# Attention in pairs of heads with plain fp32 products on halves of TensorE's array, the first block's x taken from PSUM, and two-operation bit joins

## The chip, the cores and the metric

The program runs on one core of one Trainium2 chip. The metric is the device time of one execution in microseconds. A core has five engines that work side by side and wait for each other through semaphores: PE (TensorE, the matrix products), ACT (ScalarE), DVE (VectorE), POOL (GpSimd) and SP (SyncE, which here only issues transfers). Products read SBUF and write PSUM, which has eight banks of 512 fp32 columns on 128 partitions.

## The reference

Attention for 4 batches and 8 heads over 576 positions of width 64, mixed with a memory read-out, then two feed-forward layers over 2304 rows. Inputs q, k, v are fp32, some inputs are scaled by 8, and the weights of both layers come as 64-bit floats.

```python
B, H, S, D = q.shape                                    # 4, 8, 576, 64
scores = q @ k.transpose(0, 1, 3, 2) / np.sqrt(D)       # causal mask, then softmax
a = softmax(np.where(causal, -1e9, scores))
local = a @ v
q_p = phi(q)                                            # x if x > 0 else exp(x) - 1, plus 1
mem_out = (q_p @ M_prev) / ((q_p * z_prev).sum(-1) + 1e-6)
x = g * mem_out + (1 - g) * local                       # g = sigmoid(beta), per head
x = x.transpose(0, 2, 1, 3).reshape(B * S, H * D)       # 2304 x 512
h = x @ w_in                                            # first layer, 512 x 2048
y = (s * np.maximum(h, 0) ** 2 + b) @ w_out             # 2048 x 512
h2 = y @ w_in2                                          # second layer
out = (h2 * np.tanh(softplus(h2))) @ w_out2             # 2304 x 512
```

## The kernel before

A planner in the kernel (class `Plan`) orders the work. Each step names its engine, an estimated duration, a priority, the buffers that it reads and writes, and its code. `order` plays the steps in time: each engine takes the ready step with the smallest priority number, and a step whose buffers have no free place in their ring waits. The outcome is a fixed order of instructions on every engine. While the program runs, each engine keeps that order and waits where it has to. While nothing else is ready for PE early on, the planner inserts products of zeros (`zero_product`).

Attention is done head by head (`unit`). The memory read-out is put in front of the scores: 64 columns of phi(q), divided by their norm, stand ahead of the probabilities, and M stands ahead of v, so that one weighting product does both. A head has 640 padded rows in five tiles of 128: the first half, TA, is tiles 0 to 2, the second half, TB, is tiles 3 and 4. For each tile PE makes the scores, DVE subtracts from the mask and takes the row minimum, ACT takes the exponential with its row sum, POOL, DVE or ACT scale by the reciprocal of the sum. PE then turns the tile in 128 x 128 pieces (transposes against `ident`), ACT copies the turned pieces out of PSUM, and PE weights v with them. The result goes to `x_d` in DRAM.

The eight heads of batch 0 ("early") use plain fp32 products: scores over rows 0 to 63 (L534), weighting into 64 columns (L624, 128\*64 in the rows). Their first halves come first, then their second halves. The other 24 heads split every operand into a high and a low part of type fp32r on ACT and DVE (L509 to L513, L601, L604, L646, L647), and use two full-width products for each (L538, L539, and L624 with 128\*128 in the rows); a last DVE operation adds the two halves of the result (L635).

The first layer (`first`, `y_part`) works in blocks of x: five small ones of 256 rows and two large ones of 512 (`NBIG`). Three products of fp32r parts stand for one exact product. `load_x` fetches a block of x from DRAM, ACT makes its high part, DVE its low part (L822 to L824). A small block handles two of the sixteen pieces of the hidden layer at a time. Large blocks use buffers (`m2a`) that open only when the last attention step is done. `rank1` gives the first layer priority numbers between those of the heads.

The weights come as 64-bit floats. `convert` loads a piece of 512 per partition, ACT scales the upper and the lower words, DVE shifts the one (L705), isolates a sign in 16-bit halves (L707, and a custom operation L709), and ACT and DVE cut the sum into high and low parts (L715, L718). There are 32 pieces for each layer. The second layer (`hidden`, L1009, and `out_block`, L1075) uses a seven-product scheme for blocks of 768 rows.

## Time and profile before

| | before |
|---|---|
| time, median of 3 runs | 1022.97 us (1022.23 to 1026.45) |
| profiled execution, its own time | 1022.02 us |
| span of that execution | 1020.2 us |
| PE busy | 996.6 us, 6742 products |
| DVE busy | 829.3 us |
| ACT busy | 697.7 us |
| POOL busy | 204.0 us |
| PE clock granted, mean | 0.998 of full speed |

Products are pipelined, and their ends are modelled: a row of the trace shows when a product starts and how long it is under way, and the time that one takes from PE is the distance to the next start. A plain fp32 product appears as two instructions of the same size, an fp32r product as one. The span runs from the first to the last instruction; the time of the execution has 1.8 us more.

### The profile page before, as it was taken

The numbers are of one execution on the slowest core, as the hardware profiler recorded it, in microseconds if no ns is written. First come the engines' busy times: TensorE is split into PE (matmuls) and PEld (weight loads), VectorE is DVE, ScalarE is ACT, GpSimd is POOL, SyncE is SP. The second block draws the span as 40 slices with busy tenths as digits, with TensorE's granted clock in tenths as the row PEclk, the third lists the DMA queues.
The fourth block names the chain that finished last, engine by engine and source line by source line (L and its number), as shares of the span: only waits on it lengthen the run. The fifth ranks groups of instructions, "written<-read, shape, count | busy, mean of one in ns | idle before, by whom it ended". The sixth has DMA issues, their size and how long they took to land.

```text
span 1020.2 us, 19909 instructions
## 1 busy us (share of the span) xinstructions
PE 996.6 (98%) x6742; PEld 926.6 (91%) x6742; DVE 829.3 (81%) x2308; ACT 697.7 (68%) x1511; POOL 204.0 (20%) x330
## 2 busy tenths in 40 slices
PE   6899999999999999999999999999999999999998
PEld 5668799998999999999888888899999999999998
DVE  7899899999999989976789975379965789667864
ACT  6888897788877877766779987456643466434552
POOL 6752133444333334310000000000010000100000
PEclk9999999999999999999999999999999999999999
DMA  9855553324323432217899985368677665766464
GB/s 252 219 174 164 174 161 94 105 90 120 128 85 92 129 93 87 86 37 250 263 285 312 316 266 178 136 241 267 201 281 243 219 215 191 261 218 222 145 223 170
DMA packets 88661, 188.60 MB, mean 185 GB/s; under 512 B 8432, under 2 KB 62704, under 8 KB 81264
## 3 DMA queue, kind: packets, MB, share of 16 engines
q1 hardware_dynamic: 81072, 135.95, 42.8%
q0 software_dynamic: 7056, 51.38, 14.9%
q8 instruction: 53, 0.87, 0.3%
q14 instruction: 48, 0.39, 0.1%
q10 hardware_dynamic: 432, 0.01, 0.0%
HBM read 144.32 MB, written 42.99 MB: 184 GB/s over the span
## 4 chain that ended last, share of the span: by engine, by line
PE 67%; issue 18%; DMA 5%; DVE 4%; ACT 3%; POOL 2%; SPq 0%; POOLq 0%; DVEq 0%; ACTq 0%
PE bank L801 18%; PE bank L879 18%; PE bank L1009 9%; PE bank L1075 6%; PE bank L624 6%; PE bank L596 4%; PE bank L534 2%; PE bank L538 2%; DMA x_d<-xs 2%; PE bank L539 1%; POOL Pt L569 1%; DMA woh<-wo_split_d 1%; PE bank L1250 1%; DMA woh<-wi_split_d 1%; DMA wih<-in_w_in 1%
## 5 line engine op out<-in xcount | busy, mean ns | idle before, releaser
L1075 PE MATMUL bank<-woh,S 128*128 128x256 f32 x792 | 107.4, 283 | 1.8 <-DMA woh<-wo_split_d 1.8
L1075 PEld LDWEIGHTS bank<-woh,S 128*128 128x128 f32 x792 | 100.8, 192 | 1.9 <-issue 1.9
L1075 PE MATMUL bank<-wol,S 128*128 128x256 f32 x720 | 98.1, 283 | 0.0
L552 ACT ACTIVATE Pt<-Pt,mx 128x64 f32<-128x64 f32 (+4 forms) x148 | 81.4, 551 | 22.5 <-DVE mx L543 22.4
L555 POOL TENSOR_SCALAR Pt<-ex,nm 128x64 f32<-128x64 f32 x148 | 73.3, 513 | 116.3 <-PE bank L596 44.9
L1009 PE MATMUL bank<-wi,woh 128*128 128x384 f32 x426 | 94.0, 335 | 0.3 <-DMA woh<-wi_split_d 0.3
L1075 PEld LDWEIGHTS bank<-wol,S 128*128 128x128 f32 x720 | 91.8, 192 | 0.0
L990 POOL DMA_DIRECT2D wol<-wo_split_d x17 | 9.2, 540 | 357.5 <-DVE wi L730 265.7
L1009 PE MATMUL bank<-wi,wol 128*128 128x384 f32 x294 | 76.0, 335 | 0.6 <-DMA wol<-wi_split_d 0.6
L1009 PEld LDWEIGHTS bank<-wi,woh 128*128 128x128 f32 x426 | 75.6, 188 | 1.0 <-DMA woh<-wi_split_d 0.5
L596 PE MATMUL bank<-ident,Pt 128*128 128x128 f32 x432 | 64.9, 276 | 7.1 <-POOL Pt L569 6.2
L604 DVE TENSOR_TENSOR PTl<-bank,PTh 128x128 fp32r<-128x128 f32 (+1 forms) x144 | 64.1, 481 | 3.1 <-ACT PTh L601 2.5
L543 DVE CUSTOM_DVE_ANT_0 Pt<-bank,mask 128x320 f32<-128x320 f32 (+3 forms) x148 | 59.3, 419 | 6.4 <-PE bank L534 3.1
L569 POOL TENSOR_SCALAR Pt<-Pt,rs 128x64 f32<-128x64 f32 (+2 forms) x68 | 51.9, 801 | 60.0 <-DVE rs L574 36.9
L596 PEld LDWEIGHTS bank<-ident,Pt 128*128 128x128 f32 x432 | 48.7, 140 | 13.6 <-POOL Pt L569 9.2
L601 ACT CAST PTh<-bank 128x128 fp32r<-128x128 f32 (+1 forms) x144 | 54.1, 432 | 5.9 <-PE bank L596 4.6
L1009 PEld LDWEIGHTS bank<-wi,wol 128*128 128x128 f32 x294 | 53.0, 188 | 1.1 <-DMA wol<-wi_split_d 0.9
L801 PE MATMUL bank<-xh,wi 128*128 128x256 f32 x320 | 51.2, 288 | 1.5 <-ACT xh L823 1.4
L879 PE MATMUL bank<-gh,wol 128*128 128x256 f32 x320 | 52.3, 287 | 0.0
L879 PE MATMUL bank<-gl,woh 128*128 128x256 f32 x320 | 52.2, 287 | 0.0
L879 PE MATMUL bank<-gh,woh 128*128 128x256 f32 x320 | 52.0, 285 | 0.0
L624 PE MATMUL bank<-PTh,V 128*128 128x384 f32 (+1 forms) x192 | 48.1, 278 | 0.0
(279 smaller groups left out, 2851.8 us busy)
## 6 DMA issues: line engine op xcount, KB each, us to landing
wol<-wo_split_d POOLq DMA_DIRECT2D x17, 1024.0 KB, 5.2
woh<-wo_split_d POOLq DMA_DIRECT2D x16, 1024.0 KB, 5.5
qk<-in_qk SPq DMA_DIRECT2D x24, 608.0 KB, 3.9
stage<-in_w_out SPq DMA_DIRECT2D x23, 512.0 KB, 4.7
wo_split_d<-high SPq DMA_DIRECT2D x44, 256.0 KB, 4.9
stage<-in_w_in SPq DMA_DIRECT2D x21, 512.0 KB, 5.2
stage<-wi_d SPq DMA_DIRECT2D x24, 384.0 KB, 4.7
wi_split_d<-woh SPq DMA_DIRECT2D x8, 1024.0 KB, 4.8
```

Of the source, the lines that this page charges most:

```text
L543: nc.vector.tensor_tensor_reduce(Pt[t].t[:, D + lo:D + hi], ps.t[:, :hi - lo], mask[:, SP - w + lo:SP - w + hi], -SCALE, mx.t[:, t:t + 1] ...
L552: nc.scalar.activation(Pt[t].t[:, D:w + D], Pt[t].t[:, D:w + D], AF.Exp, bias=mx.t[:, t + i:t + i + 1], scale=-1.0, accum_out=rs.t[:, t:t ...
L555: add(POOL, 0.3, lambda: nc.gpsimd.tensor_scalar(Pt[t].t[:, :D], ex.t[:, t, :], nm.t[:, t:t + 1], 1.0, op0=ALU.mult, op1=ALU.mult), [ex, n ...
L569: (nc.vector if e == DVE else nc.gpsimd).tensor_scalar(x, x, r, None, op0=ALU.mult)
L596: nc.tensor.transpose(ps.t[:, c - c0, :], Pt[t].t[:, c * P:(c + 1) * P], ident)
L601: (nc.vector.tensor_copy if dve else nc.scalar.copy)(PT[0].t[:, at_], ps.t[:, :n])
L604: nc.vector.tensor_tensor(PT[1].t[:, at_], ps.t[:, :n], PT[0].t[:, at_].bitcast(F32), op=ALU.subtract)
L624: nc.tensor.matmul(o.rearrange("p (t q) -> p t q", q=P), v, x.t[:, f[0]:f[-1] + 1:f[1] - f[0] if len(f) > 1 else 1, :], start=(c == 0 and ...
L801: nc.tensor.matmul(ph, w_at(nm, r, cc)[:, o:o + P], x_at(x, cc), start=(begin and part == 0 and cc == 0), stop=(part == 2 and cc == NCC - ...
L879: nc.tensor.matmul(acc[ec // per].t[:, (ec % per) * n:(ec % per + 1) * n], w_at(nm, fc // FPR, fc % FPR)[:, ec * P:(ec + 1) * P], t(x)[:, ...
L1009: nc.tensor.matmul(ps.t[:, :H2], w[i // 4].t[:, j, kk, i % 4], x[kk].t[:, k], start=begin and part == kk == 0, stop=part == 2 and kk == 1, ...
L1075: nc.tensor.matmul(acc[t].t[:, :DH], s.t[:, j, t * P:(t + 1) * P], x.t[:, k, q % 4], start=q == part == 0, stop=q == NQ2 - 1 and part == 2)
```

## The change

`unit` gives way to `pair`, which does one half (TA or TB) of two heads. All attention now uses plain fp32 products. The q and k of the pair's first head lie on partitions 0 to 63, those of the second on 64 to 127, and each score step issues one product for each head into its own bank (L526). The weighting writes the first head to partitions 0 to 63 and the second to 64 to 127 of one bank, product by product in turn (L603). The splits of operands and of results are gone. The halves come in the order TA of the four pairs of batch 0, and then by turns TB of one pair and TA of the pair four places on (the next batch); the first ten halves use weight buffers that are not yet needed (`PLACE`, `STAGED`), the others their own.

For TA of batch 0, ACT and DVE make the high and low part of the first 256 rows of x straight from the bank (L614, L615), and the first block of the first layer reads these; only rows 256 to 319 go to DRAM. First-layer priority numbers are now 500 and up (`RANK1`), all behind attention on PE, and zero products end with the first product of the first layer (`fill_end`). There are three small and three large blocks. The conversion joins sign, upper and lower words with two operations that each do a bit operation and a second one (L667, L669) where there were three. The reduction of phi(q) with z takes one product and one sum for two heads where each tile had an operation of its own.

```diff
-    NBIG = 2
+    NBIG = 3
@@ pair, in place of unit: scores
+                def mm(lo=lo, hi=hi, ps=ps, t=t):
+                    for i in range(2):
+                        nc.tensor.matmul(ps[i].t[:, :hi - lo], qkt(t * P, P)[rows(i)], kt(lo, hi - lo)[rows(i)], start=True, stop=True)
...
-                        nc.tensor.matmul(ps.t[:, :hi - lo], lhs, B1.t[:, lo:hi], start=True, stop=False)
-                        nc.tensor.matmul(ps.t[:, :hi - lo], lhs, B2.t[:, lo:hi], start=False, stop=True)
@@ pair: turning and weighting
+                def turn(ps=ps, tcs=tcs, i=i):
+                    for x, (t, c) in enumerate(tcs):
+                        nc.tensor.transpose(ps.t[:, x, :], at_t(i, t, c * P, (c + 1) * P), ident)
...
+        def mm():
+            for c in range(last + 1):
+                ts = [t for t in g if t >= c]
+                f = [at_[t, c] for t in ts]
+                cols = slice((ts[0] - lo_t) * P, n)
+                for i in range(2):
+                    nc.tensor.matmul(pv.t[rows(i), cols].rearrange("p (t q) -> p t q", q=P), vx()[:, i, c, :],
+                                     PT[i].t[:, f[0]:f[-1] + 1:f[1] - f[0] if len(f) > 1 else 1, :],
+                                     start=(c == 0), stop=(c == last))
...
+        if b == 0 and lo_t == 0:
+            k = N1
+            xh, xl = xs_[0][0][0], xs_[0][1][0]
+            half = Buf()
+            add(ACT, act_us(k), lambda: nc.scalar.copy(xh.t[:, p], pv.t[:, skip:skip + k]), [pv], [half], [xh])
+            add(DVE, dve_us(k), lambda: nc.vector.tensor_tensor(xl.t[:, p], pv.t[:, skip:skip + k], xh.t[:, p].bitcast(F32),
+                                                                op=ALU.subtract), [pv, half], [first_x[p]], [xh, xl])
@@ convert
-        add(DVE, 0.335, prio, lambda: nc.vector.tensor_scalar(w.t, w.t, 3, None, op0=ALU.logical_shift_left), [w], [w])
-        add(DVE, 0.335, prio, lambda: nc.vector.tensor_scalar(limbs()[:, :, 1], limbs()[:, :, 3], 0x8000, None, op0=ALU.bitwise_and),
-            [raw, low_words], [signed])
-        add(DVE, 0.75, prio, lambda: nc.vector.tensor_tensor(w.t, w.t, words()[:, :, 0], op=ALU.add), [raw, signed, w], [w])
+        add(DVE, 0.6, prio, lambda: nc.vector.scalar_tensor_tensor(words()[:, :, 0], words()[:, :, 1], -2 ** 31, words()[:, :, 0],
+                                                                   op0=ALU.bitwise_and, op1=ALU.bitwise_or), [raw, low_words], [signed])
+        add(DVE, 0.6, prio, lambda: nc.vector.scalar_tensor_tensor(w.t, w.t, 3, words()[:, :, 0], op0=ALU.logical_shift_left,
+                                                                   op1=ALU.bitwise_or), [raw, signed, w], [w])
@@ order of the halves
+    halves_ = [(0, p, TA) for p in range(H // 2)]
+    for i in range(B * H // 2):
+        halves_.append((*divmod(i, H // 2), TB))
+        if i + H // 2 < B * H // 2:
+            halves_.append((*divmod(i + H // 2, H // 2), TA))
+    for i, x in enumerate(halves_[:STAGED]):
+        pair(x[0], x[1], STEP * i, x[2], PLACE[i % len(PLACE)], i < H // 2 and i % 2 == 1)
...
-        return UNIT0 + UNIT * (i + LEAD) / PER_UNIT
+        return RANK1 + i
...
     plan.fill = (7.0, 85.0, 0.12, zero_product)
+    plan.fill_end = in_steps[0][0]
```

PE where the first layer begins, in the order before. L534 are scores, L1250 products of zeros, L624 a weighting, L801 the first layer; PTl and vx are the turned probabilities and the values of a second half of batch 0, xh is the block loaded from DRAM.

```order
L534 MATMUL bank_113<-qk_849 128x256
L1250 MATMUL bank_109<-zeros 128x256 x3
L624 MATMUL bank_112<-PTl_937,vx_831 64x256 x4
L624 MATMUL bank_112<-PTl_937,vx_831 64x128
L801 MATMUL bank_106<-xh_961,wi_196 128x256 x4
```

The same place now. L603 is the weighting of the fourth pair's first half, two heads by turns, L526 are scores of a second and of the next first half, L1215 zeros, L762 the first layer.

```order
L603 MATMUL bank_110<-PT_686,wol_0_185 64x384
L603 MATMUL bank_110<-PT_695,wol_0_185 64x384
L603 MATMUL bank_110<-PT_686,wol_0_185 64x256
L603 MATMUL bank_110<-PT_695,wol_0_185 64x256
L603 MATMUL bank_110<-PT_686,wol_0_185 64x128
L603 MATMUL bank_110<-PT_695,wol_0_185 64x128
L526 MATMUL bank_113<-qk_230 128x256
L526 MATMUL bank_111<-qk_230 128x256
L1215 MATMUL bank_109<-zeros 128x256 x4
L762 MATMUL bank_106<-xh_358,wi_219 128x256 x4
L526 MATMUL bank_112<-wih_0_350 128x192
L526 MATMUL bank_110<-wih_0_350 128x192
```

The first product of the first layer has moved from behind the weightings of all eight first halves and two second halves of batch 0 to the place right behind the fourth pair's first half.

PE in the middle of the attention before: a score step of one head (L538, L539 the two fp32r products) between first-layer products and the head's transposes (L596), all of full width.

```order
L801 MATMUL bank_107<-xh_3432,wi_196 128x256 x4
L596 MATMUL bank_113<-ident,Pt_0_3379 128x128 x3
L596 MATMUL bank_110<-ident,Pt_0_3379 128x128 x2
L538 MATMUL bank_112<-B_0_3449,A_3402 128x320
L539 MATMUL bank_112<-B_0_3467,A_3402 128x320
L538 MATMUL bank_111<-B_0_3449,A_3402 128x448
L539 MATMUL bank_111<-B_0_3467,A_3402 128x448
L801 MATMUL bank_106<-xh_3432,wi_196 128x256 x4
```

And now: transposes of the two heads (L581), first-layer products (L838, L762), scores on row halves (L526), the weighting on column halves (L603).

```order
L581 MATMUL bank_111<-ident,Pt_0_2617 128x128 x2
L581 MATMUL bank_112<-ident,Pt_1_2618 128x128 x2
L838 MATMUL bank_108<-gh_2416,wol_0_403 128x256 x2
L838 MATMUL bank_109<-gh_2416,wol_0_403 128x256 x2
L762 MATMUL bank_106<-xh_1838,wih_0_1168 128x256 x4
L526 MATMUL bank_113<-qk_2590 128x320
L526 MATMUL bank_110<-qk_2590 128x320
L603 MATMUL bank_111<-PT_2740,vx_2607 64x256
L603 MATMUL bank_111<-PT_2747,vx_2607 64x256
```

Attention steps of half rows or half columns now stand between products of full width all through the attention, where only batch 0 had such steps.

## Rows read from the trace of the kernel before

**Rows 1.** The page, part 1: busy time, share of the span, instructions.

```profile
PE 996.6 (98%) x6742; PEld 926.6 (91%) x6742; DVE 829.3 (81%) x2308; ACT 697.7 (68%) x1511; POOL 204.0 (20%) x330
```

**Rows 2.** Table by stage: start and end, length, then busy us of each engine.

```profile
core 0: us, PE busy (x) PEld busy (x) DVE busy (x) ACT busy (x) POOL busy (x), PEclk, DMA share, GB/s
0.00:63.10 63.10, 51.11 (x259) 36.24 (x259) 50.98 (x201) 48.88 (x135) 45.25 (x69) 0.97 0.78 215
...
120.00:480.00 360.00, 354.28 (x2821) 343.32 (x2821) 325.78 (x1144) 278.79 (x680) 119.33 (x192) 1.00 0.37 112
480.00:647.00 167.00, 167.00 (x759) 138.74 (x758) 125.42 (x256) 135.65 (x252) 0.00 (x0) 1.00 0.82 267
647.00:1021.00 374.00, 367.32 (x2566) 364.59 (x2564) 273.72 (x531) 185.14 (x344) 26.07 (x49) 1.00 0.64 215
```

**Rows 3.** Order of time on PE: start us, us under way, instructions merged.

```profile
63.08 1.51 PE L624 MATMUL bank<-PTl,vx 128*64 128x384 f32 x6
...
78.56 1.22 PE L801 MATMUL bank<-xh,wi 128*128 128x256 f32 x8
```

**Rows 4.** Order of time, ACT: the first split of a loaded block of x.

```profile
75.32 0.61 ACT L823 CAST xh<-xr 128x512 fp32r<-128x512 f32 x1
```

**Rows 5.** Chain that ended last, its last long pieces: start us, us, what.

```profile
902.46 54.08 PE bank L1009 x312
956.55 60.48 PE bank L1075 x504
```

**Rows 6.** Order of time on PE, first layer, small blocks and large blocks.

```profile
420.07 0.64 PE L801 MATMUL bank<-xh,wi 128*128 128x256 f32 x4
...
422.47 0.64 PE L879 MATMUL bank<-gl,woh 128*128 128x256 f32 x4
...
529.87 1.07 PE L879 MATMUL bank<-xh,woh 128*128 128x512 f32 x4
...
542.56 1.07 PE L879 MATMUL bank<-xl,wol 128*128 128x512 f32 x4
```

**Rows 7.** Order of time on PE, a later head: transposes, then a first-half weighting.

```profile
422.95 0.82 PE L596 MATMUL bank<-ident,Pt 128*128 128x128 f32 x6
423.52 0.28 PE L538 MATMUL bank<-B,A 128*128 128x64 f32 x1
...
426.75 0.33 PE L624 MATMUL bank<-PTh,V 128*128 128x384 f32 x1
...
427.51 0.69 PE L879 MATMUL bank<-gh,wol 128*128 128x256 f32 x4
```

**Rows 8.** Groups by line and shape on DVE, the joins of a conversion.

```profile
L707 DVE TENSOR_SCALAR stage<-stage 128x512 uint16<-128x512 uint16 x44 | 33.2, 763 | 2.6 <-ACT stage L703 2.5
L709 DVE CUSTOM_DVE_ANT_0 stage<-stage 128x1024 uint16<-128x1024 uint16 x37 | 25.7, 694 | 0.4
L705 DVE TENSOR_SCALAR stage<-stage 128x512 int32<-128x512 int32 x52 | 22.8, 442 | 2.4 <-ACT stage L698 2.4
```

**Rows 9.** Order of time on PE, plain heads of batch 0.

```profile
23.82 1.35 PE L534 MATMUL bank<-qk 64*128 64x64 f32 x6
25.10 0.39 PE L1250 MATMUL bank<-zeros 128*128 128x256 f32 x1
25.32 0.27 PE L596 MATMUL bank<-ident,Pt 128*128 128x128 f32 x1
25.53 1.51 PE L624 MATMUL bank<-PTl,wol 128*64 128x384 f32 x6
26.97 0.33 PE L596 MATMUL bank<-ident,Pt 128*128 128x128 f32 x1
...
64.52 1.99 PE L534 MATMUL bank<-qk 64*128 64x448 f32 x6
66.43 1.69 PE L1250 MATMUL bank<-zeros 128*128 128x256 f32 x12
...
70.23 2.16 PE L624 MATMUL bank<-PTh,wih 128*64 128x256 f32 x10
72.32 0.64 PE L534 MATMUL bank<-qk 64*128 64x448 f32 x1
```

More of the change, by code (lines that the diff above doesn't have):

```diff
@@ L430, in attention_then_two_ffn, with pair, part @@
     attention_steps = []
-    def unit(b, h, prio, groups=(TA, TB), place=None):
+    xs_ = {0: [[Buf(R[x], [P, NCC, N1], F32R)] for x in ("xh", "xl")]}
+    first_x = [Buf() for _ in range(H // 2)]
+    def pair(b, p, prio, g, place=None, apart=False):
         def add(engine, us, f, r=(), w=(), keep=(), share=1.0):
             attention_steps.append(plan.add(engine, us, prio, f, r, w, keep=keep, share=share))
-        early = place is not None and place < 5
-        first_half = groups == (TA,)
-        tiles = [t for g in groups for t in g]
-        nb = tiles[-1] + 1
-        nq = nb + 1 if early else NQ + 1
-        if early and place < 4:
-            qk_b = qn_b = vx_b = Buf(R[("wih", "wil", "woh", "wol")[place], NR - 1], [P, 2 * SP + (nq + nb) * D])
-        else:
-            qk_b, qn_b, vx_b = Buf(R["qk"], [P, SP + S]), Buf(R["qn"], [P, (NQ + 1) * D]), Buf(R["vx"], [P, NQ * D])
-        q0_ = tiles[0] * P
-        nqc, nkc = len(tiles) * P, D + P * tiles[-1]
-        k0_ = nqc
+        n_t, lo_t, last = len(g), g[0], g[-1]
+        nb = last + 1
+        nqc = n_t * P
+        nkc = nqc if lo_t == 0 else S
+        q0_ = lo_t * P
+        hs = slice(2 * p, 2 * p + 2)
+        sizes = nqc + nkc, 2 * (n_t + 1) * D, 2 * nb * D
+        if place is None:
+            qk_b, qn_b, vx_b = (Buf(R[x], [P, n]) for x, n in zip(("qk", "qn", "vx"), sizes))
+            starts = 0, 0, 0
+        else:
+            qk_b = qn_b = vx_b = Buf(R[("wih", "wil", "woh", "wol")[place], NR - 1], [P, sum(sizes)])
+            starts = 0, sizes[0], sizes[0] + sizes[1]
+        def part(x, i, t):
+            return x.t[:, starts[i]:starts[i] + sizes[i]].rearrange("p (h t d) -> p h t d", h=2, t=t)
         def qkt(a, n):
@@ new lines, in pair @@
+        add(DVE, 0.15, lambda: gate(nm.t[:, :, :n_t], 0, 1e-6), [nm], [nm])
+        add(DVE, 0.09, lambda: nc.vector.reciprocal(nm.t[:, :, :n_t], nm.t[:, :, :n_t]), [nm], [nm])
+        if apart:
+            low = [Buf(R["Pt3"], [P, 4 * P]) for _ in range(2)]
+            high = [Buf(R["Pt4"], [P, 5 * P]) for _ in range(2)]
+            Pt = {(i, t): ((low, 0), (high, 0), (high, 2 * P))[t] for t in g for i in range(2)}
+            Pt = {(i, t): (x[i], a) for (i, t), (x, a) in Pt.items()}
+        else:
+            Pt = {(i, t): (Buf(R[f"Pt{t}"], [P, P * (t + 1)]), 0) for t in g for i in range(2)}
@@ new lines, in pair, with sums, scale @@
+        gated, done = Buf(), Buf()
+        def sums():
+            return rs.t[:, :, lo_t:last + 1]
+        def scale(i, t, e):
+            x, r = at_t(i, t, D, P * (t + 1)), rs.t[:, i, t:t + 1]
+            if e == ACT:
+                nc.scalar.activation(x, x, AF.Copy, scale=r)
+            else:
+                (nc.vector if e == DVE else nc.gpsimd).tensor_scalar(x, x, r, *((None, ALU.mult) if e == DVE else (1.0, ALU.mult, ALU.mult)))
+        add(DVE, 0.15, lambda: gate(sums(), 1, 1e-9), list(rs_in.values()), [gated], [rs])
@@ L640, in unit @@
-        for t in groups[0]:
-            score(t)
-        norm(groups[0])
-        add(DMA, 0.6 * nb / NQ, lambda: nc.sync.dma_start(vx(), vm[b, h][:, :nb]), w=[vx_b])
-        if not early:
-            V = Buf(R["V"], [P, NQ, 2 * D], F32R)
-            add(ACT, act_us(NQ * D), lambda: nc.scalar.copy(V.t[:, :, :D], vx()), [vx_b], [V])
-            add(DVE, dve_us(NQ * D), lambda: nc.vector.tensor_tensor(V.t[:, :, D:], vx(), V.t[:, :, :D].bitcast(F32), op=ALU.subtract),
-                [vx_b, V], [V])
@@ L649, in unit @@
-        if len(groups) > 1:
-            for t in TB:
-                score(t)
-            weigh(TA)
-            norm(TB)
-        weigh(groups[-1])
+                add(e, us, lambda i=i, t=t, e=e: scale(i, t, e), [done, Pt_in[i, t]], [Pt_in[i, t]], [Pt[i, t][0], rs])
+        at_ = ({(0, 0): 0, (1, 1): 1, (1, 0): 2, (2, 1): 3, (2, 0): 4, (2, 2): 5} if lo_t == 0 else
+               {(t, c): 4 * (t - lo_t) + c for t in g for c in range(t + 1)})
+        order = sorted(at_, key=at_.get)
+        groups = (order[:3], order[3:]) if lo_t == 0 else (order[:4], order[4:7], order[7:])
@@ L811, in load_x @@
         big = n > N1
[L812 removed]
+        xh, xl = xs_[j] = [[Buf(R[x], [P, NCC // (1 + big), n], F32R) for _ in range(1 + big)]
                           for x in (("yh", "yl") if big else ("xh", "xl"))]
```

278 lines of the change are left out of this document (107 added, 171 removed).

## The prediction

> **What bounds the kernel now.** I read the page's busy shares first, then the table by stage, then TensorE's order of time at three places, and last the chain that ended last.
>
> The shares [rows 1] and the stages [rows 2] say one thing: TensorE is the bound from the first product of the first layer to the end. Between 120 and 480 us it is busy 354.3 of 360 us, from 480 to 647 all of 167, and in the second layer 367.3 of 374. DVE is the next engine, 325.8 of 360 us in the attention stage. So time saved on DVE, ACT or POOL counts only before TensorE is filled. What is to be seen before that: the eighth head's first-half weighting starts at 63.08 us, and the first product of the first layer at 78.56 [rows 3]. In between x goes to DRAM, comes back, and is split on ACT at 75.32 [rows 4], while TensorE runs second halves of the attention and multiplies zeros.
>
> So the time is: the start of the first layer, plus the TensorE work left then, plus waits, plus the tail. For the kernel before this closes as follows.
> - Second layer: 54.08/312 = 0.173 us for a 384-column product, 60.48/504 = 0.120 for a 256-column one [rows 5]; 1008 and 1512 of them make 174.7 + 181.4 = 356.1.
> - First layer: 0.120 for 256 columns (2.40 us for 20) and 0.2266 for 512 (12.69 us for 56) [rows 6]; 1920 and 768 of them, and ten zero starts at 0.23, make 406.8.
> - The 24 later heads, split in two fp32r products: 0.76 us for 2 x 768 columns [rows 7], so 0.0005 per column; 2 x 3520 columns are 3.5 us a head, 84 in all.
> - 414 transposes at 0.11 (six and the wait for the next in 0.57, five steps inside 0.82 - 0.27 [rows 7]) are 45.5; the remaining plain heads about 24.
>
> That is 916; 78.6 + 916 = 995, and the last product ends at 956.55 + 60.48 = 1017.0, so some 22 us are waits, spread thin. The tail to the span's end is 3.2 us, and the profiled execution lasted 1022.0, 1.8 above its span and 1.0 below the median.
>
> **The change part by part.**
>
> *Start of the first layer.* The first block's x no longer goes through DRAM: one ACT and one DVE operation take it from the bank, and the product follows. Up to there TensorE, DVE, ACT and POOL must do four pairs' first halves and eleven weight pieces. The kernel before needs 63.1 us for its eight first halves, with DVE busy 51.0, ACT 48.9 and POOL 45.3 [rows 2]: three engines near 80%, so their sum of work decides. By the order, DVE now has 36 conversion operations before that point where it had 52 by 63.1 us (13 + 14 + 13 + 12), and each piece's three joins of 0.44, 0.76 and 0.69 us [rows 8] become two. I price those two at 0.69, the nearest row of their size; nothing shows a bit operation with two operands on 32 bits, and 0.44 to 0.9 bounds it. ACT has 38 conversion operations for 41. Altogether I take a tenth off 63.1: **57 us**. Bounds: 49, if one engine's 44 us ran from 5 us without a gap, and 66, if nothing is faster and only DRAM is saved (63.1 + 1.4 for the weighting + 1 for copy and queue).
>
> *Scores and weighting.* A plain fp32 product is two passes in the trace: three score products stand as x6, and three weighting products too [rows 9]. Less the change of arrangement below, one head's first half costs 1.18 us of scores (23.82 to 25.10) and 1.34 of weighting (25.53 to 26.97), its second half 1.81 (64.52 to 66.43) and 1.99 (70.23 to 72.32). The kernel now issues two heads in turn, on row halves for the scores and on column halves for the weighting. No row shows two halves at once, since the old kernel always used rows 0 to 63 or columns 0 to 63. If the halves overlap fully, a pair costs what one head costs; if not at all, twice that. After the start, 12 first-half and 15 second-half score sets and 12 and 16 weightings are left: 14.2 + 27.2 + 16.1 + 31.8 = 89 us at the low end, 179 at the high end. I take neither end. Passes are issued in order, so the second head's first pass can begin only with the first head's second: an isolated step takes three pass times instead of two, a run of k products per head 2k + 1. Half the score steps stand alone in the order, hence 1.25 x 41.4 = 51.7, and 17.4 + 33.6 = 51.0 for the weighting: **103 us**, near the low end, because rows of half size already behave as an arrangement of their own (next item).
>
> The Trainium skill ("TensorE: Matmul & The Clock Gate", Part 3: Packing small matmuls) says that products on different tiles of the array run at the same time, with starts some 4 ns apart, and in issue order. By its starts alone this term would be 89 and the whole 983; no run here shows it yet.
>
> *Change of arrangement.* One transpose to the next costs 0.11 us, but from the transpose at 25.32 to the half-width product at 25.53 it is 0.21 [rows 9], while a transpose and a full-width product follow without it (0.57 for six) [rows 7]. So each change between full, half-row and half-column products costs 0.10. The order has 62 such changes before and 183 now, 153 of them after the start: **15 us**.
>
> *First layer.* With three large blocks 768 products of 256 columns become 384 of 512 and 1152 small ones remain: 138.2 + 261.0 + 1.4 = **400.6**, 6 us less.
>
> *The rest.* Second layer unchanged, **356.1**; 432 transposes, **47.5**. The operations taken from ACT and DVE in the attention (splits of q, k, v and the turned weights; by the order 62 DVE instructions per two heads become 31) are hidden by TensorE, whose idle time between 120 and 480 us is 5.7 us [rows 2]. The shorter conversions of the second layer's weights lie at 480 to 647 us, under a TensorE without a gap, and gain nothing. The extra small loads (z apart, two per q and k) sit in SP's queue ahead of weight pieces; half the bytes of q and k fall away, and I cost them at nothing within the bounds of the start. For waits I take **12 us** of the old 22: they sat with the 256-column products, now 1152 of 1920, and DVE is no longer at 90%. Bounds 5 and 30, since the order is fixed and twice as much of it is attention.
>
> Sum: 57 + 356.1 + 400.6 + 47.5 + 102.7 + 15.3 + 12 + 3.2 = 994.4, and 1.8 outside the span: **996 us**.
>
> **The rivals.**
> - *The halves do not overlap* (slower). Both kinds in series cost 179 instead of 103: 1072. Weighting alone (two column halves into one bank) costs 95.8 for 51.0: 1041; scores alone 82.8 for 51.7: 1027, no change. It decides from a little over a third of the overlap lost, 27 of 76 us. For it: no row shows overlap. Against: the 0.10 us at each change says that half-size products are a mode of their own.
> - *Attention outlasts the small blocks.* The large blocks' buffers open only when the last attention step is done, and only three small blocks remain, 138 us. With 165.5 us of attention TensorE is covered until 57 + 304 = 361 us. If the chain through POOL and ACT takes 30 us longer, TensorE idles for as long: 1026. Against: before, DVE held the attention, and its load is halved; POOL did only 119 us in 360.
> - *The first layer starts no earlier than the engines allow before,* 66 to 75 us, because weight loads or POOL hold the four pairs: 1005 to 1014, little gained.
>
> **How the numbers follow.** Forecast 0.70 (976 to 1012 by the bounds of start, waits and overlap), late start 0.08, halves in series 0.14 (0.03 scores only, 0.05 weighting only, 0.06 both), attention outlasting 0.05, better than 976 0.03. The range 976 to 1027 leaves out the series of the weighting and the best corner. About 0.5% (1018 to 1028) is what this measurement can tell from no change. Faster: 0.70 + 0.08 + 0.03 and some of the outlasting, 0.83; same 0.06; slower 0.11. The likeliest case alone has 980 to 1010.
>
> **What would show it.** The first product of the first layer at 50 to 65 us, right behind the fourth pair's weighting. In TensorE's order of time, a second-half weighting of a pair (x20 passes) in about 2.1 us, not 4, and a 320-column score pair in about 0.8. The attention ending before 361 us, with TensorE's idle time between the start and there under 15 us. The second layer as long as before. Wrong would be: x20 in 4 us; idle TensorE ahead of transposes, waiting for POOL; or a large block that begins only after a gap.

## The result

| | before | after |
|---|---|---|
| time, median | 1022.72 us (1022.23 to 1026.45, 4 runs) | 995.2 us (993.02 to 996.82, 4 runs) |
| after / before | | 0.9722, 95% interval 0.9691 to 0.9752 |
| profiled execution, its own time; its span | 1022.02; 1020.2 us | 996.01; 994.2 us |

The change makes the kernel 2.8% faster; 996 was forecast. One execution of a later experiment, the shared bank, took 3316.51 us; the record does not show why, and no ratio contains it. The page of after, part 1, against [rows 1]:

```profile
PE 972.1 (98%) x6342; PEld 854.8 (86%) x6342; DVE 680.9 (68%) x1638; ACT 635.5 (64%) x1361; POOL 183.2 (18%) x346
```

TensorE still has 98% of the span. DVE has lost 148 us and ACT 62, but TensorE's own busy time fell by 24.5, and the span by 26.0. The table by stage of after, cut at the first layer's first product, the large blocks and the second layer:

```profile
core 0: us, PE busy (x) PEld busy (x) DVE busy (x) ACT busy (x) POOL busy (x), PEclk, DMA share, GB/s
0.00:62.00 62.00, 49.25 (x297) 35.72 (x298) 48.33 (x146) 45.94 (x125) 44.84 (x74) 0.94 0.91 256
62.00:120.00 58.00, 57.37 (x445) 45.47 (x445) 53.51 (x167) 51.79 (x131) 26.16 (x48) 1.00 0.48 135
120.00:361.70 241.70, 238.52 (x1864) 193.15 (x1861) 175.12 (x546) 170.30 (x440) 86.12 (x177) 0.99 0.49 139
361.70:620.00 258.30, 257.90 (x1169) 214.30 (x1168) 129.47 (x250) 180.95 (x322) 0.00 (x0) 1.00 0.55 180
620.00:991.00 371.00, 369.05 (x2574) 366.16 (x2572) 274.07 (x532) 186.52 (x345) 26.10 (x49) 1.00 0.64 217
```

Against [rows 2], DVE falls from 90% to 72% of the attention stage, and the second layer is as long as before. TensorE's order of time in after: the start of the first layer (L762, against [rows 3]), a stretch of attention, and the begin of the large blocks.

```profile
60.68 0.70 PE L526 MATMUL bank<-qk 64*128 64x256 f32 x4
61.31 0.74 PE L1215 MATMUL bank<-zeros 128*128 128x256 f32 x4
61.89 0.64 PE L762 MATMUL bank<-xh,wi 128*128 128x256 f32 x4
...
199.44 0.81 PE L526 MATMUL bank<-qk 64*128 64x320 f32 x4
200.18 2.17 PE L603 MATMUL bank<-PT,vx 128*64 128x256 f32 x20
202.27 1.56 PE L526 MATMUL bank<-stage 64*128 64x448 f32 x8
203.76 0.74 PE L838 MATMUL bank<-gh,wol 128*128 128x256 f32 x4
204.34 0.64 PE L762 MATMUL bank<-xl,wi 128*128 128x256 f32 x4
...
361.72 1.09 PE L762 MATMUL bank<-yh,wi 128*128 128x512 f32 x4
```

A second-half weighting of *two* heads (x20) takes 202.27 - 200.18 = 2.09 us; one head alone took as long before (72.32 - 70.23, [rows 9]). And the first four full-width products behind a half-array step are under way for 0.74 us, the next four for 0.64: part of a change of arrangement is paid in the first product of the new kind. What TensorE still waits for in after (us in total, times, longest):

```profile
PE bank L581 <- POOL Pt L558: 6.8, 9, 2.1
PE bank L1215 <- ACT zeros L394: 4.7, 1, 4.7
PE bank L581 <- DVE Pt L558: 1.9, 1, 1.9
PE bank L1034 <- DMA woh<-wo_split_d: 1.4, 1, 1.4
```

**Where the 26 us came from.** I gave each TensorE instruction the time to the next one's start, took out gaps in which no product was under way, and summed by kind over the whole execution. Each column adds up to the start of the last product (us):

| | before | after | by head | x by load | half added | full added | two large | fewer changes |
|---|---|---|---|---|---|---|---|---|
| ahead of the first product | 6.6 | 4.7 | 4.8 | 4.9 | 4.7 | 4.6 | 4.8 | 4.8 |
| gaps | 13.8 | 14.1 | 13.0 | 11.8 | 9.1 | 15.7 | 14.1 | 13.5 |
| products of zeros | 27.7 | 23.7 | 23.7 | 28.0 | 19.6 | 18.6 | 24.8 | 24.9 |
| scores | 71.8 | 65.2 | 64.8 | 64.9 | 65.4 | 70.7 | 65.9 | 62.7 |
| transposes | 48.3 | 54.8 | 52.4 | 50.0 | 75.6 | 58.1 | 53.4 | 52.8 |
| added products | | | | | 58.8 | 31.3 | | |
| weighting | 75.6 | 58.1 | 90.3 | 58.8 | 61.8 | 58.8 | 59.7 | 57.9 |
| first layer | 416.2 | 413.4 | 413.2 | 414.0 | 412.5 | 409.6 | 419.4 | 414.8 |
| second layer | 356.8 | 356.5 | 356.5 | 356.7 | 356.4 | 356.3 | 356.4 | 356.4 |
| sum | 1016.8 | 990.5 | 1018.7 | 989.1 | 1063.9 | 1023.7 | 998.5 | 987.8 |

From before to after, weighting gives 17.5, scores 6.6, zeros 4.0, the first layer 2.8 and the time ahead of the first product 1.9; transposes take back 6.5. So the gain is TensorE work that is gone, two thirds of it (17.6 of 26.3 us) in the attention.

Not all of the 6.5 us of the transposes goes to changes of arrangement. In three stretches of 3.4 us of this execution, from 20.0, 54.1 and 149.7 us on, the granted clock was 0.50, the lower of its two levels (1.2 of 2.4 GHz). Shortly ahead of each TensorE had stood idle, for 2.14 and 0.55 us, for 1.18 and 0.67, for 0.80 and 1.88. In the third a transpose takes 0.213 us to the next start, and 0.109 just before it, so about half of such a stretch is lost. The table of that stretch (its columns as above; the clock stands third from the end) and TensorE's order of time there:

```profile
149.66:153.06 3.40, 3.40 (x18) 3.15 (x16) 3.40 (x7) 3.01 (x7) 0.00 (x0) 0.50 0.43 150
...
149.38 3.82 PE L581 MATMUL bank<-ident,Pt 128*128 128x128 f32 x18 [1.88 <-DVE Pt L558]
```

Of these stretches 5.6 us lie in transposes in after and 0.5 in before. So some 2.5 of the 6.5 us are the clock's, and about 4 are left for changes of arrangement. The execution of x by load has no such stretch, and its transposes take 50.0. The changed kernel's nine executions, five of them in the run after again below, follow the clock: 992.6 to 993.0 us in the four with a mean granted clock of 0.998, 999.25 in the one with 0.991.

### The profile page after: what moved, and what is told of

It is laid out like the page before. It is cut to its first block, busy times and chain, and to the rows that moved or that the text cites. A ratio compares the mean times of both kernels' runs of the same rounds, so it can differ in the third digit from the quotient of the medians.

```text
span 994.2 us, 18129 instructions
## 1 busy us (share of the span) xinstructions
PE 972.1 (98%) x6342; PEld 854.8 (86%) x6342; DVE 680.9 (68%) x1638; ACT 635.5 (64%) x1361; POOL 183.2 (18%) x346
## 4 chain that ended last, share of the span: by engine, by line
PE 79%; issue 7%; DMA 6%; ACT 4%; POOL 2%; DVE 1%; POOLq 0%; SPq 0%; ACTq 0%
PE bank L762 18%; PE bank L838 17%; PE bank L968 15%; PE bank L1034 13%; PE bank L581 5%; PE bank L526 5%; PE bank L603 5%; POOL Pt L558 2%; DMA wo_split_d<-high 1%; DMA woh<-wo_split_d 1%; ACT Pt L540 1%; DMA wol<-wi_split_d 1%; DMA wih<-in_w_in 1%; ACT stage L660 1%; DMA stage<-in_w_in 1%
## 5 line engine op out<-in xcount | busy, mean ns | idle before, releaser
L586 ACT COPY PT<-bank 128x384 f32<-128x384 f32 (+1 forms) x144 | 62.9, 490 | 31.2 <-PE bank L581 28.7
L543 POOL TENSOR_SCALAR Pt<-ex,nm 128x64 f32<-128x64 f32 x160 | 61.6, 404 | 112.4 <-DVE nm L500 54.1
L581 PE MATMUL bank<-ident,Pt 128*128 128x128 f32 x480 | 73.1, 284 | 9.0 <-POOL Pt L558 6.8
L532 DVE CUSTOM_DVE_ANT_0 Pt<-bank,mask 128x320 f32<-128x320 f32 (+3 forms) x160 | 64.0, 430 | 22.6 <-PE bank L526 21.6
L968 PEld LDWEIGHTS bank<-wi,woh 128*128 128x128 f32 x426 | 75.6, 188 | 0.6
L581 PEld LDWEIGHTS bank<-ident,Pt 128*128 128x128 f32 x480 | 55.7, 145 | 17.5 <-POOL Pt L558 10.4
L558 POOL TENSOR_SCALAR Pt<-Pt,rs 128x64 f32<-128x64 f32 (+2 forms) x96 | 60.5, 650 | 40.0 <-DVE rs L561 33.1
L838 PE MATMUL bank<-xh,woh 128*128 128x512 f32 x240 | 64.2, 389 | 0.0
L821 DVE TENSOR_TENSOR xh<-g,xh 128x512 fp32r<-128x512 f32 x30 | 20.6, 688 | 60.2 <-ACT xh L819 60.2
L838 PEld LDWEIGHTS bank<-xh,woh 128*128 128x128 f32 x240 | 45.0, 188 | 9.1
L762 PE MATMUL bank<-yh,wi 128*128 128x512 f32 x192 | 51.4, 391 | 0.4 <-ACT g L811 0.4
L811 ACT ACTIVATE g<-bank 128x512 f32<-128x512 f32 x48 | 28.6, 595 | 33.4 <-PE bank L762 33.4
L762 PEld LDWEIGHTS bank<-yh,wi 128*128 128x128 f32 x192 | 35.3, 188 | 7.6 <-ACT g L811 0.8
```

Source lines behind the costliest of these rows:

```text
L532: nc.vector.tensor_tensor_reduce(at_t(i, t, D + lo, D + hi), ps[i].t[:, :hi - lo], mask[:, SP - w + lo:SP - w + hi], -SCALE, mx.t[:, i, t: ...
L543: add(POOL, 0.33, lambda i=i, t=t: nc.gpsimd.tensor_scalar(at_t(i, t, 0, D), ex.t[:, i, t - lo_t, :], nm.t[:, i, t - lo_t:t - lo_t + 1], 1 ...
L558: (nc.vector if e == DVE else nc.gpsimd).tensor_scalar(x, x, r, *((None, ALU.mult) if e == DVE else (1.0, ALU.mult, ALU.mult)))
L581: nc.tensor.transpose(ps.t[:, x, :], at_t(i, t, c * P, (c + 1) * P), ident)
L586: (nc.vector.tensor_copy if dve else nc.scalar.copy)(PT[i].t[:, x:x + n], ps.t[:, :n])
L762: nc.tensor.matmul(ph, w_at(nm, r, cc)[:, o:o + P], x_at(x, cc), start=(begin and part == 0 and cc == 0), stop=(part == 2 and cc == NCC - ...
```

## The experiments

The ratio beside each is to the kernel before on the same chip.

**The weighting by head.** Does the order in which the heads are written matter?

```diff
-            for c in range(last + 1):
+            for i in range(2):
+                for c in range(last + 1):
...
-                for i in range(2):
```

> One edit: in the weighting step the products of the two heads are no longer written in turns (key tile by key tile, head 0 then head 1) but head by head: all of head 0's, then all of head 1's. Nothing is left out, the number of products and of changes of arrangement is the same. Theory: the halves overlap only because neighbouring passes belong to different halves, so the weighting's 50.9 us after the start of the first layer in the trace of after become about 95 (the passes run one behind the other), and the time is 1035 to 1050 us where weighting is on the path throughout. Rival: the two halves work from queues of their own, and the order in which they are written does not matter: 993 to 998 us.

1024.67 us, ratio 1.0035 (1.0019 to 1.0051): 29.5 us slower than after by the medians, 32 by the ratios, and the change's whole gain is gone. TensorE's order of time, a first-half and a second-half weighting of a pair:

```profile
204.12 2.21 PE L603 MATMUL bank<-PT,stage 128*64 128x384 f32 x12
...
211.07 3.51 PE L603 MATMUL bank<-PT,vx 128*64 128x256 f32 x20
```

3.51 us for the same x20, 2.21 for the x12 (1.52 in after, at 210.42), and 90.3 us of weighting in the table for 58.1. The rival is out: the order decides. Theory was right in kind and too high in price, because a part still overlaps. In the single starts of this row, head 0's passes start at 211.07, .34, .56, .77, .99, 212.20 and 212.420, and head 1's first pass at 212.425, while three more passes of head 0 wait (each head's ten end with two of 128 columns, which tells them apart). In the x12, with six passes of a head written ahead, it is the same: head 1's first pass starts at 204.825, when three of head 0 are left.

**The weighting in twos.** How far ahead does the overlap reach?

```diff
-            for c in range(last + 1):
+            for c, i in [(c, i) for c0 in range(0, last + 1, 2) for i in range(2) for c in range(c0, min(c0 + 2, last + 1))]:
```

> One edit: in the weighting step the products are written in twos: two key tiles of head 0, then the same two of head 1, and so on. Nothing is left out. In the run by head, head 1's first pass starts 5 ns behind a pass of head 0 that has three more passes of head 0 waiting behind it, and not earlier. Theory A (TensorE can start a pass of the other half past three waiting passes of the first): two products of a head are four passes, of which one runs and three wait, so the halves still overlap, the weighting takes 51 to 56 us after the first layer's start, and the time is 994 to 1000 us. Theory B (only the very next pass can start beside a running one): the halves overlap at the seams alone, and the time lies halfway to the run by head, at 1008 to 1016 us.

993.59 us, 0.9725 (0.9702 to 0.9747), as after. Its x20:

```profile
197.98 2.22 PE L603 MATMUL bank<-PT,vx 128*64 128x256 f32 x20
```

Theory A holds: two products of one head, four passes, may stand ahead of the other head's and the halves overlap in full (weighting 52.1 us after the start, 50.9 in after). Six and ten passes ahead, as in the run by head, are too many; five was not tried.

**The first block's x by a store and a load.** Is the route out of PSUM worth what the sum gave it?

```diff
-    xs_ = {0: [[Buf(R[x], [P, NCC, N1], F32R)] for x in ("xh", "xl")]}
+    xs_ = {}
...
-        if b == 0 and lo_t == 0:
+        if False:
...
-                need = [*(xl if part == 2 else xh), *first_x, W["wil" if part == 1 else "wih", r]] + [ph] * (k + part > 0)
+                need = [*(xl if part == 2 else xh), W["wil" if part == 1 else "wih", r]] + [ph] * (k + part > 0)
...
-                if j > 0:
-                    load_x(j, -1.0)
+                load_x(j, -1.0)
```

> One edit: the first block's x is again written to DRAM and loaded like the others, not copied out of PSUM into the first layer's tiles. Nothing is left out. Theory: the first layer's first product, at 61.9 us in the trace of after, has to wait for a store and a load behind the fourth pair and comes 7 to 12 us later; the time rises by as much, to 1002 to 1008 us. Rival: the start is set by the transfers of weights (the DMA queues are full from 10 to 50 us), which this does not touch, so the start moves by under 2 us and the time stays at 993 to 998 us.

995.48 us, 0.976 (0.9725 to 0.9794). The first layer starts later by far more than the theory said, and the time hardly moves: the medians are alike, the ratios 3 to 4 us apart (0.976 beside 0.9722 and 0.9727), within their intervals. The first product of its first layer in TensorE's order of time (in brackets the idle time ahead and what ended it):

```profile
77.92 0.51 PE L762 MATMUL bank<-xh,wi 128*128 128x256 f32 x2 [0.44 <-ACT xh L782]
```

And its group of zero products:

```profile
L1214 PE MATMUL bank<-zeros 128*128 128x256 f32 x165 | 29.4, 314 | 4.9 <-ACT zeros L394 4.9
```

The start moved by 16.0 us, from 61.9 to 77.9. Neither text foresaw this: not the theory (the time did not follow), nor the rival (the start did). TensorE did second halves of the attention meanwhile, which it had to do anyway: after the start, 17.6 us less work is left (911.1 against 928.7 us). What a later start costs is more zeros (4.3 us in the table). Gaps and transposes gave that back, but in part through the clock: the profiled execution of this run has the full clock throughout, that of after the lower clock for 10.2 us. At a like mean clock this run is the slower one: 1001.58 beside 999.25 us at 0.991, and 994.31 and 994.69 at 1.0, where the changed kernel has 992.6 to 993.0 at 0.998. So the route out of PSUM is worth some 2 to 4 us by an estimate from these few executions, and not the 16 us of the start. What makes the clock fall is open: TensorE waits for 2.14 us near 18.8 us in both traces, and only in after does the clock fall behind it, at 20.0 us.

**A half product, or a full one, ahead of each step of transposes.** What does a change of arrangement cost?

```diff
                 def turn(ps=ps, tcs=tcs, i=i):
+                    nc.tensor.matmul(ps.t[:, 0, :D], ident[:D], ident[:D, :D], start=True, stop=True)
```

and in the other kernel

```diff
                 def turn(ps=ps, tcs=tcs, i=i):
+                    nc.tensor.matmul(ps.t[:, 0, :D], ident, ident[:, :D], start=True, stop=True)
```

> One edit: each of the 160 steps of transposes is opened by one more plain product of 64 rows by 64 columns, which the step then overwrites. It adds work and changes no result. The product itself is two passes of 64 columns, about .1 us. Full-width steps that stood in a row now have a change to the half arrangement and one back between them. Theory A (a change of arrangement costs about .2 us to and fro, half of it in front of the first half product and half at the first full-width one): 32 to 40 us above the same product on all rows. Theory B (the .1 us that the prediction took): 12 to 18 us above it. Rival C (changes cost nothing by themselves and the gaps seen were the wait for the first operands): 0 to 3 us above it.

> The counterpart of the run with the half product: the same 160 added products, of 64 columns, but on all 128 rows, so that no arrangement changes beyond those of the changed kernel. It adds work and changes no result. Two passes of 64 columns are about .1 us each time: 160 of them are 16 us, and the time is 1008 to 1016 us by every theory; what the half product costs above this is the price of the changes.

Half: 1062.06 us, 1.0391 (1.0367 to 1.0415). Full: 1027.98 us, 1.0063 (1.0036 to 1.0089). The difference is 34.1 us, in theory A's range and far above theory B's; the traces have 468 and 182 changes, so 34.1/286 = 0.12 us each net, while gaps shrank by 6.6. The rows of transposes and added products alone differ by 45.0, or 0.16 each. The clock has a part in this: the profiled execution with the half product has the lower clock for 34.1 us in total, that with the full product for 10.2. With half of these stretches taken off, the sums of the table differ by some 28 us, and by 35 without the gaps, which is 0.12 for each change. The executions with a mean clock of 0.995 lie 31 to 33 us apart (1060.1 beside 1026.86 and 1029.1), at the edge of theory A's range. The half product in TensorE's order of time, behind four products of the first layer:

```profile
155.28 0.64 PE L763 MATMUL bank<-xl,wih 128*128 128x256 f32 x4
155.84 0.43 PE L580 MATMUL bank<-ident 64*128 64x64 f32 x2
156.21 0.55 PE L582 MATMUL bank<-ident,Pt 128*128 128x128 f32 x3
```

The full product in the other kernel, behind four products of the first layer too:

```profile
153.87 0.64 PE L763 MATMUL bank<-xh,wih 128*128 128x256 f32 x4
154.35 0.33 PE L580 MATMUL bank<-ident 128*128 128x64 f32 x2
154.51 0.61 PE L582 MATMUL bank<-ident,Pt 128*128 128x128 f32 x4
```

Start to start, the four first-layer products take 0.56 ahead of a half and 0.48 ahead of a full product; the added product 0.37 and 0.16. With the first transpose's 0.166 for 0.115 in the single starts, that is 0.08 + 0.21 + 0.05 = 0.34 us for two changes. The full run missed its own expectation (1008 to 1016): an added product with two passes costs 0.196 us in the table, not 0.1.

**Three-operation joins.**

```diff
...
-        add(DVE, 0.6, prio, lambda: nc.vector.scalar_tensor_tensor(words()[:, :, 0], words()[:, :, 1], -2 ** 31, words()[:, :, 0],
-                                                                   op0=ALU.bitwise_and, op1=ALU.bitwise_or), [raw, low_words], [signed])
-        add(DVE, 0.6, prio, lambda: nc.vector.scalar_tensor_tensor(w.t, w.t, 3, words()[:, :, 0], op0=ALU.logical_shift_left,
-                                                                   op1=ALU.bitwise_or), [raw, signed, w], [w])
+        add(DVE, 0.335, prio, lambda: nc.vector.tensor_scalar(w.t, w.t, 3, None, op0=ALU.logical_shift_left), [w], [w])
...
+        add(DVE, 0.335, prio, lambda: nc.vector.tensor_scalar(limbs()[:, :, 1], limbs()[:, :, 3], 0x8000, None, op0=ALU.bitwise_and),
+            [raw, low_words], [signed])
+        add(DVE, 0.75, prio, lambda: nc.vector.tensor_tensor(w.t, w.t, words()[:, :, 0], op=ALU.add), [raw, signed, w], [w])
```

> One edit: the joins of the weights' bits go back to three VectorE operations in place of two. Nothing is left out. Theory: the run with x by a load has shown that TensorE fills a later start of the first layer with attention; VectorE has room behind that (35.9 of 40 us busy in 80 to 120 us of the changed kernel, 95 of 140 later), so two-operation joins are worth nothing that can be measured: 993 to 998 us. Rival: ahead of the start every engine is full (VectorE 44.6 of 58 us), the conversions come later, TensorE runs more of its filling zero products, and the time rises by 3 to 6 us, to 998 to 1002 us.

996.41 us, 0.9743 (0.9724 to 0.9762), beside 0.9722 and 0.9727 of after: in the theory's range, and not to be told apart from after. By the ratios the shorter joins are worth some 2 us, which is less than the intervals can tell. The scale of ACT's operation on the lower words (L665) goes back with them.

**Two large blocks.**

```diff
-BANKS = [("y0", "y1")] * 3 + [("o0", "o1", "o2", "o3"), ("y0", "y1", "o2", "o3"), ("o0", "o1", "o2", "o3")]
+BANKS = [("y0", "y1")] * 5 + [("o0", "o1", "o2", "o3"), ("y0", "y1", "o2", "o3")]
...
-    NBIG = 3
+    NBIG = 2
...
```

> One edit: five blocks of 256 columns and two of 512 in the first layer, as before the change, in place of three and three ... that is, one large block less and two small ones more. Nothing is left out. Theory: attention ends at 337 us and the small blocks already reach to 361, so more of them hide nothing more; they cost what their products cost: 768 of 256 columns at .120 us in place of 384 of 512 columns at .227, 92.2 for 87.2 us, so the time rises by 4 to 7 us, to 999 to 1003 us. Rival: the waits on TensorE around the change of block size (2 us) and the joint load of the large blocks' x go away, and the time stays at 993 to 997 us.

The blocks' PSUM banks, and the order in which they come free, go back with the number. 1004.41 us, 0.9827 (0.981 to 0.9844): 9 to 11 us above after. The sign is the theory's, the size is above its 4 to 7. In the table the first layer takes 6.0 more and the zero products, starts of blocks among them, 1.1; the rest is not settled.

**Trying for more: the shared bank, later weights, scaling on ACT, fewer changes.** Four kernels aim at the changes of arrangement, the first 60 us and the wait for GpSimd. The core of the edits, in this order:

```diff
+            score_steps = [[(0, 0, 0, D, 0), (1, 0, 0, D + P, D)], [(2, 0, 0, D + 2 * P, 0)]]
...
-        convert(1, 3.0 * i if i < 8 else 28.0 + 3.0 * (i - 8), *p, raws[i])
+        convert(1, (3.0 * i if i < 4 else 20.0 + 2.0 * (i - 4)) if i < 8 else 40.0 + 3.0 * (i - 8), *p, raws[i])
...
-E_NORM = 'PPPDD'
+E_NORM = 'PAPDD'
...
+                    end = self.pe_end(now, got.us + CHANGE * ((got.form or "F") != form), got.share)
```

> One edit: the scores of the first two query tiles of a pair (64 and 192 columns) are one step and share one PSUM bank for each head, so there are 16 half-array steps fewer. Nothing is left out. Changes of arrangement go from 183 to 161 by the written order. Theory (a change costs about .17 us, as the pair of runs with 64-row and 128-row products shows: .09 ahead of the first product of the other kind and .05 to .1 in that product): 22 times .17 is 3.7 us, and 16 first passes at .1 less are 1.6 more: 989 to 992 us. Rival: the minimum and exponential of the first tile start later, a pair takes longer, TensorE waits or fills, and the time stays at 994 to 997 us.

> Two edits: the scores of the first two query tiles in one step, as in the run with a shared bank, and the conversions of the fifth and later pieces of the first layer's weights ordered later (rank 20 in place of 12 for the fifth, 40 in place of 28 for the ninth). Nothing is left out. Zero products that fill TensorE fall from 136 to 119 by the written order. Theory: the DMA queues are full from 10 to 50 us, fewer transfers of weights in that stretch bring the fourth pair's operands sooner, and 17 to 25 zero products less at .16 us are 3 to 4 us on top of the shared bank's: 985 to 989 us. Rival: what the pairs gain the weights lose, the first layer's later rows wait for weights, and the time is that of the shared bank alone or 2 to 4 us above it.

> One edit: the scaling of the second query tile's weights (256 columns, two heads, 16 pairs) goes from GpSimd to ScalarE, so GpSimd has four scalings in a row for each first half of a pair in place of six. Nothing is left out. In the trace of the changed kernel TensorE waits 6.8 us in nine pieces for a scaling on GpSimd, which takes .32 to 1.37 us for the same kinds of tiles. Theory: these waits shrink to under 3 us, the granted clock's drops go with them, and the time falls by 3 to 7 us, to 988 to 992 us. Rival: ScalarE is as full there (64 of 80 us), TensorE waits for it instead, and the time stays at 993 to 998 us.

> Three edits meant to make the changed kernel faster, nothing left out: the shared bank for the scores of the first two query tiles; the planner counts .17 us for a change of arrangement and, between ready steps whose ranks lie within 15, takes the one that needs no change; the scaling of the first query tile goes from GpSimd to ScalarE and that of the second to VectorE. Changes of arrangement go from 183 to 148 by the written order. Theory: 35 changes at .17 us are 6 us, less waiting for GpSimd 3 us: 985 to 989 us. Rival: as with the shared bank alone, what the changes save comes back as waits and zero products in the first 80 us: 991 to 995 us.

> The changed kernel once more, with no edit, so that the three other runs of this call stand beside it on the same chip: 993 to 998 us, 0.970 to 0.975 of the kernel before.

| | median us | ratio to before (95%) |
|---|---|---|
| after again | 992.65 | 0.9727 (0.9703 to 0.9751) |
| shared bank | 993.49 | 0.9721 (0.9705 to 0.9737) |
| shared bank, later weights | 997.95 | 0.9761 (0.9732 to 0.9789) |
| scaling on ACT | 994.41 | 0.9733 (0.971 to 0.9756) |
| fewer changes | 994.4 | 0.9735 (0.9716 to 0.9754) |

None is faster than the changed kernel beyond what the intervals allow; in each of the four the time came nearest to the rival's.

For the shared bank the mechanism was not the rival's. Gaps and zero products take 13.1 and 24.0 us there, 14.1 and 23.7 in after. But its profiled execution has the clock at 0.50 for 17.1 us, and after for 10.2. Its four executions at a mean clock of 0.991 to 0.993 took 993.4 to 994.3 us, where the changed kernel took 999.25 at 0.991; so at a like clock it is the faster one by some 5 us, about what its theory had said. With the later weights too the time follows the clock: 0.50 for 30.7 us of its profiled execution, 992.75 us at a mean of 0.993 and 1003.35 at 0.986. Whether the edits themselves bring the lower clock is not shown.

The waits of the run with scaling on ACT show a part of why its theory failed:

```profile
PE bank L581 <- POOL Pt L558: 2.2, 2, 2.0
PE bank L526 <- DVE stage L669: 2.2, 1, 2.2
PE bank L968 <- DMA wol<-wi_split_d: 1.2, 1, 1.2
```

The wait for GpSimd fell from 6.8 to 2.2 us as meant, gaps by 2.4, and changes after the start rose from 153 to 160, zero products from 136 to 141. In the run with fewer changes scores and transposes fell by 4.5 us (some 1.7 of it the clock's, in the transposes), first layer and zeros rose by 2.6. Runs of the changed kernel itself lie between 992.6 and 999.3, and most of that follows the clock, so effects of 2 to 3 us stay open.

## Why the prediction was right, and where not

*Bound by TensorE.* Right: the second layer, the large blocks and the attention run with TensorE busy 98.7 to 99.8%.

*The sum.* Its terms against the trace of after, counted from the first layer's start; "taken" marks what is the forecast's own:

| term | forecast | measured |
|---|---|---|
| start of the first layer | 57 | 61.9 |
| second layer | 356.1 | 356.5 |
| first layer and its zero starts | 400.6 | 401.8 (138.2 of it taken) |
| transposes | 47.5 | 47.5 (taken) |
| scores and weighting | 102.7 | 89 (the low end, taken) |
| changes of arrangement | 15.3 | 27.9 (the rest) |
| waits | 12 | 6.0 |
| tail | 3.2 | 3.5 |

The rows give only the sum of small-block products, transposes, scores and weighting, 302.6 us without waits. With 138.2 for the first, 47.5 for the second and 89 for the overlapped attention, 27.9 are left for 153 changes. This rest is only as good as what was taken. The transposes were read too high: six in 0.57 us [rows 7] are 0.095 each and not 0.11, and the 414 behind the start of the first layer took 40.9 us in before, 0.099 each. At that price 432 take 42.7, and the trace's 47.4 hold changes and the lower clock besides.

*Scores and weighting: the step that failed.* "An isolated step takes three pass times instead of two, a run of k products per head 2k + 1" is wrong, and so is its ground, that the second head's first pass can begin only with the first head's second. The trace has first pass of head 0, first pass of head 1 some 6 to 7 ns later, then both second passes (199.439, 199.446, 199.812 and 199.819 us for the pair of score products below): a run takes 2k pass times. A 320-column score pair takes 200.18 - 199.44 = 0.74 us with the change behind it, a second-half weighting of two heads 2.09. So the low end of 89 was the value. (By the rule itself the scores were priced too low: 56 of the 80 score steps after the start stand alone and 24 in twos, so with steps counted as alike it asks for about 1.43 times 41.4, an estimate of 59 us and not 51.7.) Here the rule weighed in the prediction (the Trainium skill, "TensorE: Matmul & The Clock Gate", Part 3: Packing small matmuls) was the better guide: it has starts about 4 ns apart, and the trace agrees but for 2 to 3 ns. The prediction's "in issue order" does not hold throughout: in the run by head a pass of head 1 starts ahead of three passes of head 0 that were written before it.

*Changes of arrangement: mis-sized.* 0.10 each was taken, which is the gap ahead of the first product (0.09 to 0.10). The other part, 0.05 to 0.10 in the first product of the new kind, was not seen: the rows of the kernel before that were read ended at the gap. By the rest of the sum a change costs 0.18, or 0.20 with the transposes at 42.7 and the 1.7 us that the lower clock cost behind the start taken off; 0.17 in the single starts beside the half product; 0.12 by the two kernels with added products. What lies between is open; all lie above the 0.10 taken. The Trainium skill ("TensorEngine Tiling (Array Packing)", Key Properties) says that a change of mode drains TensorE and gives no price. The trace has a price at each change; the drain itself no run here shows, since the ends of products are modelled. The error in the changes and the one in the scores and weighting, 12.6 too little and 13.7 too much, cancel, and so nearly do those of the start (4.9 too little) and the waits (6.0 too much): that the forecast came within 1 us is luck.

*The start.* 61.9 lies within its bounds of 49 to 66, but the term stands for less than it seems. The sum let it fall by 21.6 us, most of it because x no longer goes through DRAM; the run with x by a load has it at 77.9 and nearly the same time. A later start is filled with attention, so only zeros, gaps and the time ahead of the first product count: 48.1 us before, 42.5 after, 44.7 with x by a load. The route out of PSUM is worth 2 to 4 us by the estimate above.

*The clock.* The prediction has no term for it. It was at the lower level for 10.2 us in the execution of after, and about 5 us were lost by that, 1.7 of them behind the start of the first layer.

*Joins.* The two new operations take 698 and 695 ns, as priced from [rows 8] at 0.69 (groups by line of after, DVE):

```profile
L667 DVE SCALAR_TENSOR_TENSOR stage<-stage 128x512 int32<-128x512 int32 x44 | 30.5, 698 | 10.5 <-ACT stage L665 10.3
L669 DVE SCALAR_TENSOR_TENSOR stage<-stage 128x512 int32<-128x512 int32 x37 | 25.6, 695 | 1.4 <-ACT stage L660 1.0
```

*The large block.* 6 us were forecast for it; taking it back costs 9 to 11.

*The rivals.* Halves in series: not in after, but the run by head shows how near it lies, since the loss of 29.8 of the weighting's 47.9 us of overlap brings the time of before back, close to the 27 us at which the prediction let it decide. Attention outlasting the small blocks: its last weighting ended at 337.7, and the large blocks began at 361.7, where the prediction had put the end of the cover (361). First layer no earlier than 66: no.

## What to carry to other kernels

Where two products use halves of TensorE's array, write them in turns: the order in which they stand decided over the whole gain here (in twos is as good, by head is not). When an engine is full, sum its work by kind over the whole run and count only waits and filler ahead of a milestone; an earlier milestone gains little if other necessary work was done before it. Before two runs a few us apart are compared, look at the granted clock of each. Read the price of a change of mode up to the second product behind it, not only to the first.

## What the hardware showed that I had not expected

- Passes of fp32 products on two halves start 6 to 7 ns apart, with both heads' second passes behind both first ones. A pass was seen to start beside a running one past three waiting passes of the other half; with six or ten passes of one head written ahead (the run by head), the rest ran in series.
- A change between full and half arrangement shows in two places, 0.08 to 0.10 us ahead of the first product and 0.05 to 0.10 in it.
- The granted clock of one and the same kernel differs from execution to execution (0.991 to 0.998), and the time with it (999.25 to 992.6 us).
- The second pass of a full-height product with 64 columns takes 0.11 us ahead of a transpose, as long as a transpose of 128 columns; its first pass 0.06 (single starts of the run with the full product). What sets this was not tried.
